# One high half of the split FFN weights made by VectorE instead of ScalarE

## The chip, the cores and the metric

The program runs on one core of one Trainium2 chip. Five engines work from queues of their own, each in the order of its queue: PE (TensorE, matmuls), DVE (VectorE), ACT (ScalarE), POOL (GpSimd) and SP (SyncE, which here only issues DMAs). An instruction that must wait for another engine or for a transfer holds up everything behind it on its own engine. The metric is the device time of one execution in microseconds (us), as the median of several runs.

## The reference

Four layers run over a sequence of 2048 rows of 512 columns: a state-space convolution and a gated feed-forward network (FFN), twice, each behind a layer norm and with a residual. All weights are float32 and shared by the two passes.

```
x = A_u
for _ in range(2):
    x = x + conv(layernorm(x))      # K[d, l] = Re sum_n C dt B exp(dt A l); causal FFT convolution, + u * Dskip
    x = x + ffn(layernorm(x))       # (silu(x @ w_gate) * (x @ w_up)) @ w_down, F = 1376
return x
```

## The kernel before

The sequence is cut into four blocks of 512 rows. The convolution kernel K is built in eight chunks of 64 columns (`gen_exp`, `gen_trig`, `gen_g`, `gen_e`, then the matmuls of `lags`, L496 and L497), taken to the frequency domain by matmuls (`spectra`, `first_parts`, `later_parts`) and kept as `w0r` for the first part and in DRAM (`wdr`) for the later ones. `ssm_half` multiplies a block's spectrum by it on DVE (L781, L784 into `yk`, then L786 and L787 into `yf`), turns the product back on PE (`pi`, L803), combines the pieces on ACT and DVE (`bb`, L753, L761, L762) and adds the result to the block (`xg`). The FFN then runs on PE over pairs of columns of F (`pgu`, L916 to L919, in two buffers; L883 to L885 for the last 96 columns), with ACT making silu (`sg`, L922), DVE the product with the up part (L923, which gives the `pgu` buffer free), ACT and DVE the two halves of the result (`hh` L924, `hl` L925), and PE the product with w_down (`py`, L931 to L933), which DVE adds to the block (L936).

The FFN multiplies in float16. So each weight is split once into two float16 tiles: a high half, the scaled weight rounded, and a low half, the scaled weight less the high half. `split_weights` (L652 to L700) makes lists of three kinds of step from eight pieces of w_gate and w_up (a quarter of the columns, 128 x 4 x 344, named by `j` = 0..3 and `wi` = 0 for gate, 1 for up) and eleven pieces of w_down: `load` issues the DMA into a float32 tile (`st`, or a part of `wsl`), `hi` makes the high half on ACT (L664 for gate and up, L689 for w_down), `lo` the low half on DVE (L669 and L692) from the loaded tile and the high half. The scales `sc6` are powers of two from the largest column norms; `scales()` computes them in a chain of small DVE instructions, of which L356 is the last.

What sets the order: from the start of the program up to the line `pscale = product_scale()` the instructions of PE, DVE, ACT and POOL stand in the order in which the code emits them (`tc.manual_schedule`). The end of that stretch, printed here, mixes the split with the last two chunks of K, the convolution of block 0 (`conv[0]` for the first 256 columns, `conv[1]` for the others; each `take` of one is a product on DVE and its turn back on PE) and the first norm (`first_norm`). `split(a, b)` emits the next `a` high halves, then the next `b` low ones. Behind that line, and for the DMA queue SP in parts of it too, a list scheduler that plays the program through with its own durations decides the order; a change in the stretch ahead can move everything behind it.

```
scales()
split(1, 0)              # hi of (j 0, gate)
first_parts(c, 0)        # PE L580, then ACT L581: w0r of q = 0
take(conv[0], 1)
split(1, 1)              # hi of (j 0, up), lo of (j 0, gate)
split(0, 0, 1)
first_parts(c - 1, 3)    # w0r of q = 3
split(1, 0)
take(conv[0], 1)
```

Of the kernel before, what the change touches and what calls it, by code (L numbers as in the profile page):

```python
# [15 lines left out]
AF = mybir.ActivationFunctionType  # L16
OP = mybir.AluOpType
# [57 lines left out]
def kernel(ctx, tc, x, a_re, a_im, b_re, b_im, c_re, c_im, log_dt, d_skip,  # L75
                           w_gate, w_up, w_down, c_ef, c_ei, c_ek, c_am, c_eh, c_eih, out):
    nc = tc.nc
    V, A, G, PE = nc.vector, nc.scalar, nc.gpsimd, nc.tensor
# [9 lines left out]
    def tl(shape, name, tag, dt=F32):  # L88
        return sb.tile(shape, dt, name=name, tag=tag, bufs=BUFS[tag])
# [544 lines left out]
    def wgu(wi, kc, lo, n=1):  # L634
        u = 8 * wi + 4 * lo + kc
        v = wsl[u // 6].rearrange("p (u f) -> p u f", u=6)
        return v[:, u % 6] if n == 1 else v[:, u % 6:u % 6 + n]

    def wd(fc, lo):
        r = 2 * fc + lo  # L640
        if r < 5:
            return wsl[2][:, 4 * F + r * D:4 * F + (r + 1) * D]
        return wsl[3][:, (r - 5) * D:(r - 4) * D] if r < 21 else wx

    def split_weights():


        cb = F // 4
        tags = iter(("bt", 0, 1, 2, "bt", 0, 1, 2, "n", "xf", "bt"))

        def columns(j, wi, src):
            fs = slice(j * cb, (j + 1) * cb)  # L652
            sc = sc6[:, wi:wi + 1]
            at = []

            def load():
                tag = next(tags)
                st = tl([P, 4, cb], "st2", tag) if isinstance(tag, str) else \
                    wsl[3].bitcast(F32)[:, 4 * cb * tag:4 * cb * (tag + 1)].rearrange("p (k f) -> p k f", k=4)
                nc.sync.dma_start(st, src[:, fs].rearrange("(k p) f -> p k f", p=P))  # L660
                at.append(st)

            def hi():
                A.activation(wgu(wi, 0, 0, 4)[:, :, fs], at[0], AF.Copy, scale=sc)  # L664

            def lo():
                n = 2 if wi == 0 else 4
                for k in range(0, 4, n):
                    V.scalar_tensor_tensor(wgu(wi, k, 1, n)[:, :, fs], at[0][:, k:k + n], sc,  # L669
                                           wgu(wi, 0, 0, 4)[:, k:k + n, fs], OP.mult, OP.subtract)  # L670
            return load, hi, lo

        def rows4(f0):
            n = min(4, F // P - f0)
            at = []

            def part(fc):
                rows = min(P, F - fc * P)
                sc = sc6[:rows, 2:3]

                def load():
                    st = tl([P, min(4, FT - f0), D], "st3", next(tags))
                    nc.sync.dma_start(st[:, :n], w_down[f0 * P:(f0 + n) * P].rearrange("(k p) d -> p k d", p=P))
                    if f0 + n < FT and n < 4:
                        nc.sync.dma_start(st[:F % P, n], w_down[(f0 + n) * P:])
                    at.append(st)

                def hi():
                    A.activation(wd(fc, 0)[:rows], at[0][:rows, fc - f0], AF.Copy, scale=sc)  # L689

                def lo():
                    V.scalar_tensor_tensor(wd(fc, 1)[:rows], at[0][:rows, fc - f0], sc, wd(fc, 0)[:rows],  # L692
                                           OP.mult, OP.subtract)
                return load if fc == f0 else None, hi, lo
            return [part(fc) for fc in range(f0, min(FT, f0 + 4))]

        parts = [columns(j, wi, src) for j in range(4) for wi, src in enumerate((w_gate, w_up))]
        for f0 in range(0, FT, 4):
            parts += rows4(f0)
        return [p[0] for p in parts if p[0]], [p[1] for p in parts], [p[2] for p in parts]  # L700
# [583 lines left out]
```

## Time and profile before

| what | value |
|---|---|
| median of 3 runs | 1151.85 us (1150.62 to 1154.33) |
| the profiled execution, its own time | 1153.06 us |
| its span, first to last instruction | 1151.3 us |
| instructions | 24412 |
| mean granted TensorE clock | 0.992 |

The page gives each engine's busy time and share of the span, the span in 40 slices, the chain of work that ended last and the costliest groups. The answers of the trace that the prediction shows are of four kinds. A row of the waits names who waited, for whom, and then the microseconds in total, how often, and the longest. A row of the timeline has the start in us, the duration, engine, line, operation, tiles written and read, shapes, how many instructions it merges, and in brackets the idle time before it with what ended it. A row of the groups by line gives, behind the bar, busy us and mean ns of one. A row of the windows gives, for a stretch of time, its length, then the busy time of PE, weight loads, DVE, ACT and POOL with counts, the granted clock of PE (1.00 is full speed), the DMA engines' share and GB/s. Times in the timeline count from the span's start; PE ends are modelled.

### The profile page before, as it was taken

How to read it: one execution, taken by the hardware profiler on the slowest of the kernel's cores; microseconds unless marked ns; L12 is line 12 of the kernel's file. 1: busy time of each engine (PE TensorE's matmuls, PEld its weight loads, DVE VectorE, ACT ScalarE, POOL GpSimd, SP SyncE). 2: the span in 40 equal slices, each digit the busy share in tenths (PEclk: the TensorE clock that was granted, in tenths of full speed). 3: DMA queues.
4: the chain of work that ended last, by engine and by line, in shares of the span. 5: the costliest groups of instructions: out<-in, count | busy, mean ns of one | idle time of the engine just before them, and what ended most of it. 6: DMA issues, size and time to landing. Idle time of an engine off the chain costs nothing.

```text
span 1151.3 us, 24412 instructions
## 1 busy us (share of the span) xinstructions
PE 1097.2 (95%) x9942; PEld 874.7 (76%) x9942; DVE 998.3 (87%) x1585; ACT 598.1 (52%) x1198; POOL 108.6 (9%) x163
## 2 busy tenths in 40 slices
PE   2989999999989999999999999999999999999998
PEld 1868888888875868686868687877778687876875
DVE  8999999988999899998999999989994999973211
ACT  6989998734454453567453534655434352334211
POOL 0112222210000100111010000110000100000000
PEclk9989999999989999999999999999999999999999
DMA  5367777868773355332354444334443156302000
GB/s 210 128 166 166 162 185 172 191 174 300 223 197 98 105 143 192 115 96 71 107 142 138 133 140 151 109 117 114 139 133 129 50 134 156 103 32 48 14 24 19
DMA packets 127314, 150.38 MB, mean 131 GB/s; under 512 B 50897, under 2 KB 75985, under 8 KB 127202
## 3 DMA queue, kind: packets, MB, share of 16 engines
q1 hardware_dynamic: 115298, 123.32, 35.6%
q0 software_dynamic: 11904, 25.50, 9.5%
q8 instruction: 78, 1.28, 0.5%
q14 instruction: 34, 0.28, 0.1%
HBM read 98.70 MB, written 33.82 MB: 115 GB/s over the span
## 4 chain that ended last, share of the span: by engine, by line
PE 39%; DVE 25%; issue 6%; DMA 2%; ACT 2%; POOL 1%; DVEq 0%; POOLq 0%; ACTq 0%
PE pgu L916 7%; PE pgu L917 7%; PE pgu L919 7%; PE py L931 4%; PE py L932 4%; PE py L933 4%; DVE yk L784 3%; DVE t L781 3%; PE pi L803 3%; DVE yk L781 3%; PE pf L280 2%; DMA mix<-nn 2%; DVE z L228 2%; DVE sg L923 2%; DVE hl L925 2%
## 5 line engine op out<-in xcount | busy, mean ns | idle before, releaser
L916 PE MATMUL pgu<-mix,wsl 128*128 128x256 f16 x1280 | 299.7, 273 | 5.6 <-DVE sg L923 4.7
L917 PE MATMUL pgu<-mix,wsl 128*128 128x256 f16 x1280 | 299.4, 273 | 0.0
L919 PE MATMUL pgu<-mix,wsl 128*128 128x256 f16 x1280 | 195.7, 273 | 0.0
L917 PEld LDWEIGHTS <-wsl 128*128 128x128 f16 x1280 | 125.5, 98 | 22.5 <-issue 6.2
L931 PE MATMUL py<-wsl,hh 128*128 128x512 f16 (+1 forms) x352 | 134.2, 381 | 7.0 <-DVE xg L936 5.3
L916 PEld LDWEIGHTS <-wsl 128*128 128x128 f16 x1280 | 125.5, 98 | 16.4
L919 PEld LDWEIGHTS <-wsl 128*128 128x128 f16 x1280 | 125.4, 98 | 14.8
L933 PE MATMUL py<-wsl,hl 128*128 128x512 f16 (+1 forms) x352 | 133.9, 381 | 0.0
L932 PE MATMUL py<-wsl,hh 128*128 128x512 f16 x320 | 122.0, 381 | 0.0
L781 DVE TENSOR_TENSOR t<-uu,w 128x1024 f32<-128x1024 f32 x96 | 117.0, 1218 | 0.2
L784 DVE TENSOR_TENSOR yk<-yk,t 128x1024 f32<-128x1024 f32 x96 | 116.9, 1218 | 0.2
L922 ACT ACTIVATE sg<-pgu,sc 128x512 f32<-128x512 f32 x80 | 54.6, 683 | 119.8 <-PE pgu L919 113.5
L923 DVE SCALAR_TENSOR_TENSOR sg<-pgu,sc,sg 128x512 f32<-128x512 f32 x80 | 59.7, 746 | 52.0 <-ACT sg L922 51.8
L924 ACT ACTIVATE hh<-sg 128x512 f16<-128x512 f32 x80 | 50.1, 627 | 80.6 <-DVE sg L923 80.6
L531 PE MATMUL pw<-kt,ek 128*128 128x256 f32 (+1 forms) x384 | 91.1, 374 | 0.0
L803 PE MATMUL pi<-yl,mix 128*128 128x256 f16 x576 | 78.9, 272 | 1.3 <-ACT yl L792 1.0
L531 PEld LDWEIGHTS pw<-kt,ek 128*128 128x128 f32 x384 | 72.6, 193 | 8.7
L280 PE MATMUL pf<-z,eh 128*128 128x256 f16 x576 | 74.9, 273 | 0.6 <-DVE z L228 0.6
L781 DVE TENSOR_TENSOR yk<-u,w0r 128x1024 f32<-128x1024 f32 x56 | 68.2, 1218 | 0.8 <-ACT u L282 0.8
L932 PEld LDWEIGHTS <-hh 128*128 128x128 f16 (+1 forms) x352 | 34.6, 98 | 44.1 <-issue 8.7
L496 PE MATMUL pk<-re,g 128*32 128x64 f32 x1024 | 65.1, 317 | 2.8 <-DMA g<-g 1.9
L925 DVE TENSOR_TENSOR hl<-sg,hh 128x512 f16<-128x512 f32 x80 | 54.8, 686 | 14.8 <-ACT hh L924 14.8
(238 smaller groups left out, 2158.7 us busy)
## 6 DMA issues: line engine op xcount, KB each, us to landing
uu<-udr SPq DMA_DIRECT2D x96, 256.0 KB, 3.0
w<-wdr SPq DMA_DIRECT2D x96, 256.0 KB, 2.7
udr<-u POOLq DMA_DIRECT2D x32, 256.0 KB, 2.7
g<-g POOLq DMA_DIRECT2D x6, 1024.0 KB, 9.0
udr<-u SPq DMA_DIRECT2D x16, 256.0 KB, 2.9
n<-xdr SPq DMA_DIRECT2D x4, 1024.0 KB, 5.6
kdr<-ks SPq DMA_DIRECT2D x6, 512.0 KB, 2.6
kt<-kdr SPq DMA_DIRECT2D x24, 128.0 KB, 3.0
```

The costliest lines, as they stand in the source:

```text
L280: PE.matmul(pf[:, o], lhsT=e, rhs=m, start=k == 0, stop=k == len(terms) - 1)
L531: PE.matmul(pw[:, i], lhsT=e, rhs=kt[:, :, c + 4 * k0:4 * k1:4, :].rearrange("p g k d -> p k g d"), start=c == 0, stop=c == 3)
L781: V.tensor_tensor(t, uu.unsqueeze(2).to_broadcast([P, NQ, 2, 2, DC]), w.unsqueeze(3).to_broadcast([P, NQ, 2, 2, DC]), OP.mult)
L784: V.tensor_tensor(yk, yk, t, OP.add)
L803: PE.matmul(pi[:, o], lhsT=e, rhs=m, start=k == 0, stop=k == len(terms) - 1)
L916: PE.matmul(o, lhsT=wgu(wi, k, 0)[:, fs], rhs=nh[:, k], start=k == 0, stop=False)
L917: PE.matmul(o, lhsT=wgu(wi, k, 1)[:, fs], rhs=nh[:, k], start=False, stop=False)
L919: PE.matmul(o, lhsT=wgu(wi, k, 0)[:, fs], rhs=nlo[:, k], start=False, stop=k == 3)
L923: V.scalar_tensor_tensor(sg, pgu[:, 1], sc6[:, 4:5], sg, OP.mult, OP.mult)
L931: PE.matmul(py[:, r], lhsT=hh[:n, f, rc], rhs=wd(f, 0)[:n], start=f == 0, stop=False)
L932: PE.matmul(py[:, r], lhsT=hh[:n, f, rc], rhs=wd(f, 1)[:n], start=False, stop=False)
L933: PE.matmul(py[:, r], lhsT=hl[:n, f, rc], rhs=wd(f, 0)[:n], start=False, stop=f == FT - 1)
```

## The change

The high half of the first piece (j = 0, gate) is no longer an ACT activation with a scale but one DVE multiplication of the loaded tile by the same scale; the other seven pieces of gate and up and all of w_down stay on ACT. The values are the same: a power of two times the weight, rounded to float16.

```diff
             def hi():
-                A.activation(wgu(wi, 0, 0, 4)[:, :, fs], at[0], AF.Copy, scale=sc)
+                if j == 0 and wi == 0:
+                    V.tensor_scalar(wgu(wi, 0, 0, 4)[:, :, fs], at[0], sc, None, OP.mult)
+                else:
+                    A.activation(wgu(wi, 0, 0, 4)[:, :, fs], at[0], AF.Copy, scale=sc)
```

The code grows by three lines, so a line behind L664 has a number that is three higher in the changed kernel (L781 becomes L784, L923 becomes L926). In the rows below, `x128x4x344` and the like are the shapes written.

DVE, behind the chain of the scales, before (`sc_92` are the scales, `st_2529` the loaded piece, `wsl_2661` and `wsl_2662` the tiles of the halves):

```order
L356 TENSOR_SCALAR sc_92<-bits 128x6
L781 TENSOR_TENSOR yk<-mix,w0r 128x1024
L786 TENSOR_TENSOR yf<-yk 128x256
L787 TENSOR_TENSOR yf<-yk 128x256
L669 SCALAR_TENSOR_TENSOR wsl_2661<-st_2529,sc_92,wsl_2661 128x2x344
L669 SCALAR_TENSOR_TENSOR wsl_2662<-st_2529,sc_92,wsl_2661 128x2x344
```

and now:

```order
L356 TENSOR_SCALAR sc_92<-bits 128x6
L665 TENSOR_SCALAR wsl_2661<-st_2529,sc_92 128x4x344
L784 TENSOR_TENSOR yk<-mix,w0r 128x1024
L789 TENSOR_TENSOR yf<-yk 128x256
L790 TENSOR_TENSOR yf<-yk 128x256
L672 SCALAR_TENSOR_TENSOR wsl_2661<-st_2529,sc_92,wsl_2661 128x2x344
L672 SCALAR_TENSOR_TENSOR wsl_2662<-st_2529,sc_92,wsl_2661 128x2x344
```

One instruction is put in directly behind the scales, ahead of the third product of `conv[0]`. On ACT the activation between the copy of K (L525) and the copy of the first `w0r` (L581) is gone; the rest of ACT's order in the stretch written by hand is kept.

Behind that stretch the scheduler's order changes too. DVE at the first FFN groups, before, directly behind `bb<-bb,pi` (L761; `bb` is a piece of block 1's convolution, `pi` its second turned-back product, `sg` the product of the first FFN group):

```order
L784 TENSOR_TENSOR yk<-yk,t 128x1024
L614 TENSOR_TENSOR sy<-sy,dmax 1x1
L228 SCALAR_TENSOR_TENSOR xg<-bb_2671,xg 128x256
L228 SCALAR_TENSOR_TENSOR xg<-t_3009,xg 128x256
L692 SCALAR_TENSOR_TENSOR wsl_2664<-st_3056,sc_92,wsl_2664 128x512
L669 SCALAR_TENSOR_TENSOR wsl_2661<-wsl_2664,sc_92,wsl_2661 128x2x344
L669 SCALAR_TENSOR_TENSOR wsl_2662<-wsl_2664,sc_92,wsl_2661 128x2x344
L600 TENSOR_TENSOR wos<-pw,wos 128x2x3x64
L669 SCALAR_TENSOR_TENSOR wsl_2663<-wsl_2664,sc_92,wsl_2662 128x4x344
L600 TENSOR_TENSOR wos<-pw,wos 128x2x3x64
L762 TENSOR_TENSOR bb<-bb,pi 128x512
L923 SCALAR_TENSOR_TENSOR sg_3086<-pgu,sc_92,sg_3086 128x512
```

and now:

```order
L695 SCALAR_TENSOR_TENSOR wsl_2664<-st_3056,sc_92,wsl_2664 128x512
L834 TENSOR_TENSOR bb_2671<-bb_2671 128x256
L926 SCALAR_TENSOR_TENSOR sg_3086<-pgu,sc_92,sg_3086 128x512
L835 TENSOR_TENSOR t_3009<-t_3009,t_3010 128x256
L764 TENSOR_TENSOR bb<-bb,pi 128x512
L787 TENSOR_TENSOR yk<-yk,t 128x1024
L228 SCALAR_TENSOR_TENSOR xg<-bb_2671,xg 128x256
L228 SCALAR_TENSOR_TENSOR xg<-t_3009,xg 128x256
L672 SCALAR_TENSOR_TENSOR wsl_2661<-wsl_2664,sc_92,wsl_2661 128x2x344
```

The first `sg` product moves from behind the low halves to a place ahead of `bb<-bb,pi`, and so does the first low half of w_down (L692). The second `sg` product stays behind the low halves, the two `wos` and `t`; the third, which stood behind the two `hl` rows, `nn` and a `yk`, now stands ahead of all of these but one `hl`.

PE, where that `pi` is made. Before it stood inside the first FFN group:

```order
L919 MATMUL pgu<-mix,wsl_2661 128x256
L803 MATMUL pi<-yf_2955,mix 128x256
L919 LDWEIGHTS wsl_2661
L919 MATMUL pgu<-mix,wsl_2661 128x256
L803 MATMUL pi<-yf_2955,mix 128x256 x3
```

Now it stands behind the end of the first group, one matmul into the second:

```order
L922 MATMUL pgu<-mix,wsl_2662 128x256
L806 MATMUL pi<-yf_2955,mix 128x256
L919 LDWEIGHTS wsl_2661
L919 MATMUL pgu<-mix,wsl_2661 128x256
L806 MATMUL pi<-yf_2955,mix 128x256 x3
```

It moved by 14 FFN matmuls. In the same way the third `pi` moved from inside the third group to behind it, and the fourth to behind the group of the last columns. ACT, at the end of block 0's kernel work, before (`ks<-kt` is L607, the last reader of the tile whose place the second load of w_down takes):

```order
L598 ACTIVATE wos<-w0r 128x64
L753 ACTIVATE bb<-pi 128x512
L599 ACTIVATE wos<-pw 128x2x64
L598 ACTIVATE wos<-w0r 128x64
L599 ACTIVATE wos<-pw 128x2x64
L607 ACTIVATE ks,wsum<-kt_429 128x1024
L689 ACTIVATE wsl_2664<-st_3056,sc_92 128x512
```

and now:

```order
L599 ACTIVATE wos<-pw 128x2x64
L607 ACTIVATE ks,wsum<-kt_429 128x1024
L756 ACTIVATE bb<-pi 128x512
L692 ACTIVATE wsl_2664<-st_3056,sc_92 128x512
L925 ACT_TABLE_LOAD
L925 ACTIVATE sg_3086<-pgu,sc_92 128x512
```

The copy `bb<-pi` went from ahead of L607 to behind it. Further on, the order differs in many small places on all engines.

## The prediction

> **What bounds the kernel now.** I read the page's engines first, then the busy time by stretches, then PE's waits ahead of the stretch that is full. The waits are those of the 110 us from 256 to 366, where the moved work lies.
>
> ```profile
> PE 1097.2 (95%) x9942; PEld 874.7 (76%) x9942; DVE 998.3 (87%) x1585; ACT 598.1 (52%) x1198; POOL 108.6 (9%) x163
> 366.00:1008.00 642.00, 634.30 (x5341) 494.04 (x5339) 603.19 (x1008) 302.89 (x586) 50.23 (x62) 1.00 0.42 123
> 1010.00:1138.00 128.00, 127.65 (x1046) 96.19 (x1043) 45.18 (x74) 34.77 (x64) 1.80 (x4) 1.00 0.09 25
> PE pgu L916 <- DVE sg L923: 4.7, 1, 4.7
> PE py L931 <- DVE xg L936: 2.3, 1, 2.3
> PE pt L850 <- ACT nn L848: 2.3, 1, 2.3
> PE pi L803 <- DVE yf L786: 1.2, 1, 1.2
> 320.90:327.80 6.90, 5.12 (x23) 3.67 (x23) 6.90 (x14) 6.72 (x13) 0.70 (x1) 0.51 0.44 135
> 361.90:365.30 3.40, 3.40 (x9) 1.21 (x9) 3.40 (x7) 3.37 (x11) 0.16 (x1) 0.50 0.42 114
> ```
>
> PE carries the end. Behind 366 it is busy 634.30 of 642.00 us, then 127.65 of 128.00; little can be saved or hidden there, and a shift of PE at 366 reaches the end nearly whole. Ahead of it PE stands still four times for DVE or ACT: 1.2, 2.3, 4.7 and 2.3, together 10.5 us. Two of the waits are followed by a stretch at half clock (0.51 for 6.9 us with 5.12 busy, 0.50 for 3.4). At half clock half of the busy time is lost: 2.5 and 1.7 us. So 10.5 + 4.2 = 14.7 us is all that any change of order here can win.
>
> **The instruction itself.** First the rows that price it, then those beside its place.
>
> ```profile
> 254.37 0.17 DVE L356 TENSOR_SCALAR sc<-bits 128x6 int32<-128x6 int32 x1
> 241.67 0.37 SPq L660 DMA_DIRECT2D st<-in_B_w_gate_dram  x1
> st<-in_B_w_gate_dram SPq DMA_DIRECT2D x2, 688.0 KB, 9.0
> L382 DVE TENSOR_SCALAR th<-ft 128x448 int32<-128x448 f32 x1 | 0.4, 394 | 0.0
> L382 DVE TENSOR_SCALAR th<-ft 128x64 int32<-128x64 f32 x1 | 0.2, 195 | 0.0
> 262.88 1.78 DVE L669 SCALAR_TENSOR_TENSOR wsl<-st,sc,wsl 128x688 f16<-128x688 f32 x2 [6.37 <-ACT wsl L664]
> 261.41 1.43 ACT L664 ACTIVATE wsl<-st,sc 128x1376 f16<-128x1376 f32 x1
> ```
>
> The piece was asked for at 241.67 and lands some 9.0 us later, near 250.7, ahead of the scales, which are done at 254.5. So the new instruction starts behind L356 at once. The trace has none of 128 x 1376 with one scale. The two L382 rows give 199 ns for 384 more elements, 0.52 ns each; from 195 ns at 64 that is 0.87 us at 1376. Dearer is two passes of L669 over 688 elements each, 1.78 us together. I take 0.87, the same kind of operation. Either way **the cost is nothing**: DVE stood for 6.37 us ahead of L669, and even 1.78 fits. Without that cover it would be 0.9 to 1.8 us on DVE. ACT's 1.43 us falls away; that gains nothing by itself, as ACT's next copy waits for PE (`[1.27 <-PE pw L580]`, below).
>
> **What DVE gains in the stretch written by hand.**
>
> ```profile
> 260.35 1.99 PE L803 MATMUL pi<-yf,mix 128*128 128x256 f32 x8
> 264.11 0.28 ACT L581 ACTIVATE w0r<-pw 128x128 f32<-128x128 f32 x1 [1.27 <-PE pw L580]
> 266.57 0.68 DVE L761 TENSOR_TENSOR bb<-bb,pi 128x512 f32<-128x512 f32 x1
> 267.73 0.37 ACT L581 ACTIVATE w0r<-pw 128x256 f32<-128x256 f32 x1
> 267.89 1.22 DVE L781 TENSOR_TENSOR yk<-mix,w0r 128x1024 f32<-128x1024 f32 x1
> 270.00 1.23 DVE L781 TENSOR_TENSOR yk<-mix,w0r 128x1024 f32<-128x1024 f32 x1
> ```
>
> L669 needed the high half until 262.88; now both of its parts run behind `yf`, at 257.4 to 259.1, the next `yk` and `yf` to 261.0, and DVE waits for the turned-back product (PE is done with it at 260.35 + 1.99 = 262.34) instead of for ACT. `bb` is done at 263.7, not 267.2. But the two next `yk` need the `w0r` copies, which hang on PE: the one at 267.89 can start at 264.11 + 0.28 = 264.4, the one at 270.00 not ahead of 267.73 + 0.37 = 268.1. So of the 6.4 us **1.9 us remain**, 270.00 less 268.1. Behind that DVE runs without a gap to the norm of block 0; the wait of 1.2 us for `yf` goes, that of 2.3 for `nn` starts and ends 1.9 sooner: PE, ACT and DVE are all 1.9 us ahead at 301. SP's next gate load and the load of `xg` go out sooner too; neither is waited for here.
>
> **What the new order makes of it.** First ACT and SP, then DVE, then PE.
>
> ```profile
> 306.66 0.60 ACT L753 ACTIVATE bb<-pi 128x512 f32<-128x512 f32 x1 [2.73 <-DVE t L228]
> 307.61 1.07 ACT L607 ACTIVATE ks<-kt 128x1024 f32<-128x1024 f32 x1
> 308.84 0.38 SPq L683 DMA_DIRECT2D st<-in_B_w_down_dram  x1
> 314.23 0.72 ACT L689 ACTIVATE wsl<-st,sc 128x512 f16<-128x512 f32 x1 [5.46 <-DMA st<-in_B_w_down_dram]
> 314.97 1.28 ACT L922 ACT_TABLE_LOAD   x1
> 316.26 0.69 ACT L922 ACTIVATE sg<-pgu,sc 128x512 f32<-128x512 f32 x1
> 313.98 0.68 DVE L761 TENSOR_TENSOR bb<-bb,pi 128x512 f32<-128x512 f32 x1
> 316.45 0.73 DVE L692 SCALAR_TENSOR_TENSOR wsl<-st,sc,wsl 128x512 f16<-128x512 f32 x1
> 321.89 0.73 DVE L923 SCALAR_TENSOR_TENSOR sg<-pgu,sc,sg 128x512 f32<-128x512 f32 x1
> 335.85 0.73 DVE L923 SCALAR_TENSOR_TENSOR sg<-pgu,sc,sg 128x512 f32<-128x512 f32 x1
> 340.13 0.69 DVE L869 TENSOR_TENSOR nn<-nn 128x512 f16<-128x512 f32 x1 [1.75 <-DMA mix<-nn]
> 358.97 1.22 DVE L784 TENSOR_TENSOR yk<-yk,t 128x1024 f32<-128x1024 f32 x1
> 360.44 0.68 DVE L761 TENSOR_TENSOR bb<-bb,pi 128x512 f32<-128x512 f32 x1
> 361.04 0.74 DVE L936 SCALAR_TENSOR_TENSOR xg<-py,sc,xg 128x512 f32<-128x512 f32 x1
> 317.38 0.60 PE L919 MATMUL pgu<-mix,wsl 128*128 128x256 f16 x4
> 332.12 0.27 PE L916 MATMUL pgu<-mix,wsl 128*128 128x256 f16 x1
> 337.36 0.21 PE L883 MATMUL pgu<-wsl,mix 128*128 128x96 f16 x1
> ```
>
> ACT: L607 stood behind `bb<-pi`, which waited 2.73 for DVE. Ahead of it, and 1.9 sooner, it ends near 304.6; so the w_down load goes out at 304.75 instead of 308.84. With the 314.23 − 308.84 = 5.4 us that it took, it lands at 310.15. Then come L689 0.72, the table load 1.28, silu 0.69 and the first L923 0.73: done near 313.65, where before it was 322.6.
>
> PE: the second group, with `pi` ahead of most of it, ends near 316.0 (317.98 less the 1.9). The third then starts at once: the wait of 4.7 is gone and the half clock with it. A group takes 337.36 − 332.12 = 5.24; the third ends at 321.2, a `pi` and 1.1 of wait for its `yf` follow, the fourth runs 324.35 to 329.6 (before, 332.12 to 337.36).
>
> DVE decides how much of it stays. L761 starts at 314.0 as before, now behind L692 and the first L923. Before, 21.87 gapless us lay from 313.98 to the third L923 at 335.85. Moved out of them are L692 and a L923 (0.73 each), one `yk` (1.22), one `nn` and one `hl` (0.69 each) and some 0.2 of small ones: 4.2, less about 0.07 for each big row, since a row starts that much ahead of its forerunner's end (360.44 + 0.68 against 361.04): 3.9. So the third L923 runs at 332.0 to 332.75, and PE, ready at 329.6, gets **a new wait of 3.1 us** at L883. PE is 4.6 ahead there. From the third L923 to L936, 25.19 us before, 2.4 of the moved rows come in and 2.34 go (L784, a `t` and L761 now stand behind L936: 361.04 − 358.97 = 2.07, and a small one of 0.27), and the wait of 1.75 for the transposed `nn` changes by −0.3 to +0.4. L936 starts at 357.3 to 358.0, and `py` goes on near 358.05 instead of 361.84: **3.8 us ahead**, behind a wait of 2.4 as before. I take 0.4 less for a load that lands a little later than its forerunner, since DVE is held by it one to one: **3.4 us** at 366.
>
> In this execution's own time that is 1153.06 − 3.4 = 1149.7. It lies 1.2 above the median; the step is the same from the median, 1151.85 − 3.4 = **1148.4**, the forecast.
>
> [...] Half clock came behind a wait of 4.7, but also behind one of 2.3, as the windows show. [...]
>
> **The rivals.**
>
> ```profile
> x<-in_A_u_dram SPq DMA_DIRECT2D x1, 1024.0 KB, 9.8
> ```
>
> - *More is kept* (0.27). [...] Were the 1.9 won, and the 4.7, 2.5, 2.3 and 1.7 gone as well, the gain is 13.1 and the time 1138.7. Against that: DVE's rows between the third L923 and L936 stay as many as they were.
> - *The new wait brings half clock* (0.10). It starts at 332.75 and costs 1.7 to 2.5, say 2.0, as far as the wait of 2.4 behind it does not swallow it: 1151.85 − 3.4 + 2.0 = 1150.4.
> - *Given back* (0.10). Behind 362 both PE and DVE are full and the order differs in many places; if DVE or a transfer there sets the pace (DVE is busy 603.19 of 642.00), or the instruction does not free DVE because the piece lands late, the time stays 1151.85.
> - *The load of w_down holds DVE: slower* (0.08). L692 and the first L923 now stand ahead of the chain of `bb`, `yk` and the low halves, so a late landing delays all of it. The first 3.4 us of delay behind 310.15 use up the gain, and some 0.4 more is lost in the wait: the point is a landing at 314.0, 9.3 us behind its issue. The largest time for 1024 KB in the trace is 9.8: landing at 314.55, DVE 0.55 late, the wait at L883 7.5 us long and half clock of 2.5 behind it: 1151.85 + 0.55 + 2.5 = 1154.9. Against it: the same load took 5.4 four microseconds later.
>
> **How the numbers follow.** The forecast has 0.45, with gains of 2.4 to 4.6 us (1147.2 to 1149.5). The range reaches up to 1153.0, over "given back" and half way into the slower case, and down to 1143.5, over the smaller half of "more is kept". The price of the instruction, 0.87 or 1.78, moves nothing. 0.3% is 3.5 us, about what a measurement of this kernel can tell from no change. The forecast lies on that line, so half of it, 0.22, is faster, with 0.26 of "more is kept": 0.48. The rest, 0.23 + 0.01 + 0.10 + 0.10, is 0.44 within 0.3%; 0.08 is slower.
>
> **What would show it.** In the changed kernel's trace: the new row on DVE at about 0.87 us and no wait of 6.4 for ACT; `pt` of block 0's norm 1.9 us sooner, at 293.0; the w_down load issued near 304.8 and landed near 310; no 4.7 at the third group and clock 1.00 from 320 to 328; instead a wait of about 3 at the last columns' group (L886 now) for a product `sg`; `py` going on near 358. The prediction fails if DVE is held by another wait in the 1.9, if that load lands behind 313, if clock 0.5 stands behind 332, or if PE shows new waits behind 366.

## The result, and the profile after

| | before | after |
|---|---|---|
| median | 1153.51 us (1150.62 to 1155.47, 6 runs) | 1148.82 us (1147.92 to 1149.88, 6 runs) |
| ratio after / before | | 0.9961 (95% interval 0.9946 to 0.9977) |
| the profiled execution: time, span | 1153.06, 1151.3 us | 1149.31, 1147.5 us |

The kernel is 4.5 us faster (0.39%, interval 2.7 to 6.2 us). The forecast was 1148.4, a gain of 3.4 from the 1151.85 that three runs had given. Over six runs the kernel before has 1153.51, so the time was met more closely than the gain.

First the page's engines, the stretch that is full, and PE's waits from 250 to 366 in the changed kernel, in the same form as before.

```profile
PE 1095.6 (95%) x9942; PEld 874.1 (76%) x9942; DVE 998.9 (87%) x1586; ACT 596.5 (52%) x1197; POOL 113.6 (10%) x163
366.00:1008.00 642.00, 634.23 (x5372) 495.14 (x5371) 606.63 (x1012) 303.57 (x587) 53.51 (x62) 1.00 0.42 124
PE pi L806 <- DVE yf L789: 3.6, 2, 3.1
PE pgu L886 <- DVE sg L926: 3.0, 1, 3.0
PE pt L853 <- ACT nn L851: 1.9, 1, 1.9
PE pgu L919 <- DVE sg L926: 0.7, 1, 0.7
PE py L934 <- DVE xg L939: 0.7, 1, 0.7
```

PE has as much to do as before and the stretch behind 366 is as full. The waits ahead of it are 9.9 us together, where they were 10.5: the 4.7 for `sg` is down to 0.7, but 3.0 stand at the last columns and 3.1 at a `pi`. By that list hardly anything was won. The gain shows in the times, here from DVE, PE, SP and ACT of the changed kernel (timeline rows; for lines behind L664 the number of before is three lower).

```profile
254.39 0.94 DVE L665 TENSOR_SCALAR wsl<-st,sc 128x1376 f16<-128x1376 f32 x1
262.54 0.69 DVE L764 TENSOR_TENSOR bb<-bb,pi 128x512 f32<-128x512 f32 x1 [1.57 <-PE pi L806]
264.51 1.23 DVE L784 TENSOR_TENSOR yk<-mix,w0r 128x1024 f32<-128x1024 f32 x1 [0.56 <-ACT w0r L581]
268.21 1.23 DVE L784 TENSOR_TENSOR yk<-mix,w0r 128x1024 f32<-128x1024 f32 x1 [1.69 <-ACT w0r L581]
293.08 1.36 PE L853 MATMUL pt<-ident,nn 128*128 128x128 f32 x8 [1.89 <-ACT nn L851]
302.84 0.44 SPq L727 DMA_DIRECT2D eh<-in_c_eh_dram  x1
304.81 0.38 SPq L686 DMA_DIRECT2D st<-in_B_w_down_dram  x1
313.38 0.72 ACT L692 ACTIVATE wsl<-st,sc 128x512 f16<-128x512 f32 x1 [7.89 <-DMA st<-in_B_w_down_dram]
314.14 0.75 DVE L695 SCALAR_TENSOR_TENSOR wsl<-st,sc,wsl 128x512 f16<-128x512 f32 x1 [2.42 <-ACT wsl L692]
316.14 0.75 DVE L926 SCALAR_TENSOR_TENSOR sg<-pgu,sc,sg 128x512 f32<-128x512 f32 x1 [0.91 <-ACT sg L925]
335.15 0.74 DVE L926 SCALAR_TENSOR_TENSOR sg<-pgu,sc,sg 128x512 f32<-128x512 f32 x1
359.65 0.38 PE L934 MATMUL py<-wsl,hh 128*128 128x512 f16 x1 [0.67 <-DVE xg L939]
468.54 0.74 DVE L939 SCALAR_TENSOR_TENSOR xg<-py,sc,xg 128x512 f32<-128x512 f32 x1
```

The new row is there, and DVE's wait of 6.4 us for ACT is three waits of 1.6, 0.6 and 1.7 for PE and the `w0r` copies: `pt` starts 1.8 us sooner (294.88 before). The load goes out 4.0 us sooner, but ACT gets its tile at 313.38, 8.6 us behind the issue instead of 5.4, and DVE stands for it twice. So the third `sg` is only 0.7 us sooner than before and `py` goes on 2.2 sooner. One block further, at the first `xg` behind `py`, the lead is 4.4. In the kernel before, the load of `eh` and that `xg` stood here:

```profile
303.90 0.38 SPq L724 DMA_DIRECT2D eh<-in_c_eh_dram  x1
...
472.94 0.74 DVE L936 SCALAR_TENSOR_TENSOR xg<-py,sc,xg 128x512 f32<-128x512 f32 x1
```

Between `py` and that `xg` lies the stretch at half clock of before from 361.9 on (0.50, PE busy for all 3.4 us), which cost PE 1.7 us; in this execution of the changed kernel the clock is full there (1.00 from 358 to 366 and from 366 to 1008).

### The profile page after: what moved, and what is told of

The parts are those of the page before. It is cut to its first block, busy times and chain, and to the rows that moved or that the text cites. A ratio compares the mean times of both kernels' runs of the same rounds, so it can differ in the third digit from the quotient of the medians.

```text
span 1147.5 us, 24410 instructions
## 1 busy us (share of the span) xinstructions
PE 1095.6 (95%) x9942; PEld 874.1 (76%) x9942; DVE 998.9 (87%) x1586; ACT 596.5 (52%) x1197; POOL 113.6 (10%) x163
## 4 chain that ended last, share of the span: by engine, by line
DVE 33%; PE 25%; issue 9%; DMA 4%; ACT 3%; POOL 1%; SPq 1%; DVEq 0%; ACTq 0%; POOLq 0%
DVE t L784 5%; DVE yk L787 4%; PE pgu L919 4%; PE pgu L920 4%; PE pgu L922 4%; DVE z L228 3%; DVE yk L784 3%; PE py L934 3%; PE py L935 3%; PE py L936 3%; DVE sg L926 2%; DVE hl L928 2%; PE pi L806 2%; DMA mix<-nn 2%; DVE bb L228 1%
## 5 line engine op out<-in xcount | busy, mean ns | idle before, releaser
L936 PE MATMUL py<-wsl,hl 128*128 128x512 f16 (+1 forms) x352 | 133.4, 379 | 0.0
L784 DVE TENSOR_TENSOR t<-uu,w 128x1024 f32<-128x1024 f32 x96 | 116.8, 1216 | 0.2
L926 DVE SCALAR_TENSOR_TENSOR sg<-pgu,sc,sg 128x512 f32<-128x512 f32 x80 | 59.6, 745 | 53.0 <-ACT sg L925 52.9
L531 PE MATMUL pw<-kt,ek 128*128 128x256 f32 (+1 forms) x384 | 91.0, 374 | 0.0
L531 PEld LDWEIGHTS pw<-kt,ek 128*128 128x128 f32 x384 | 72.5, 193 | 8.6
L784 DVE TENSOR_TENSOR yk<-u,w0r 128x1024 f32<-128x1024 f32 x56 | 68.1, 1215 | 0.0
```

Of the source, the lines that this page charges most:

```text
L531: PE.matmul(pw[:, i], lhsT=e, rhs=kt[:, :, c + 4 * k0:4 * k1:4, :].rearrange("p g k d -> p k g d"), start=c == 0, stop=c == 3)
L784: V.tensor_tensor(t, uu.unsqueeze(2).to_broadcast([P, NQ, 2, 2, DC]), w.unsqueeze(3).to_broadcast([P, NQ, 2, 2, DC]), OP.mult)
L926: V.scalar_tensor_tensor(sg, pgu[:, 1], sc6[:, 4:5], sg, OP.mult, OP.mult)
L936: PE.matmul(py[:, r], lhsT=hl[:n, f, rc], rhs=wd(f, 0)[:n], start=False, stop=f == FT - 1)
```

## The experiments

The scheduler answers every edit with another order. So all but the op's two places are held in these kernels: each names, for every engine, its instructions in the order of the kernel before or of the changed one, and neighbours in it get a dependency that orders them and waits for nothing.

```diff
+    for engine, names in ORDER:
+        for a, b in zip(names, names[1:]):
+            tc.add_manual_dep(b, a, mybir.DependencyInfo(mybir.DependencyClass.NoSync, ...))
```

Single rows can then be moved by hand. Lines in these kernels are numbered as in the kernel before. Ratios are to runs of the kernel before on the same chip; 0.001 is 1.15 us. Runs 1 to 4, 5 to 8 and 9 to 12 were on one chip each.

| run | ratio | 95% interval | `py` goes on: its `xg` starts at |
|---|---|---|---|
| the change | 0.9961 | 0.9946 to 0.9977 | 358.86 |
| 1 op alone | 0.9978 | 0.9969 to 0.9987 | 358.44 |
| 2 order alone | 0.9977 | 0.9967 to 0.9986 | 359.37 |
| 3 DVE rows behind | 0.9937 | 0.9926 to 0.9949 | 355.85 |
| 4 `eh` behind | 0.9938 | 0.9924 to 0.9951 | 356.32 |
| 5 L607 back | 0.9979 | 0.9970 to 0.9988 | 359.30 |
| 6 `sg` early | 0.9973 | 0.9962 to 0.9984 | 358.00 |
| 7 op three times | 0.9972 | 0.9962 to 0.9983 | 357.56 |
| 8 both | 0.9954 | 0.9942 to 0.9967 | 356.83 |
| 9 the change again | 0.9963 | 0.9951 to 0.9976 | 358.05 |
| 10 op nine times | 1.0004 | 0.9995 to 1.0013 | 362.67 |
| 11 `eh` late | 0.9950 | 0.9937 to 0.9962 | 355.93 |
| 12 third `sg` early | 0.9952 | 0.9938 to 0.9966 | 357.18 |

Before, that `xg` starts at 361.04 in the profile.

### 1 and 2: the op without the order, the order without the op

```diff
 # 1: hi() as in the changed kernel
-ORDER of the changed kernel
+ORDER of the kernel before
 # 2: hi() as in the kernel before
-ORDER of the kernel before
+ORDER of the changed kernel
```

> The change's one instruction, with every other instruction of every engine held in the order of the kernel before. The prediction's first step alone: DVE and PE 1.9 us ahead at 301 (pt of the first norm near 293.0), the w_down load issued 1.9 sooner (near 306.9), the 4.7 us wait at the third FFN group still there. [...] Rival (the gain is the new order's alone): 0 to 0.5 us faster.

> The high half back on ACT as before, with every other instruction of every engine held in the order of the changed kernel. Theory (the parts add up): pt of the first norm at 294.9 as before, the w_down load issued near 306.7, no wait of 4.7 at the third FFN group, no half clock behind 320; about 2 us faster than before, 1.9 slower than the changed kernel. Rival (the order gains only where DVE has been freed): no faster than before.

The op alone is 2.5 us faster (interval 1.5 to 3.6), where the prediction's first step has 1.9, the order alone 2.7 (1.6 to 3.8); together 5.2, and the change has 4.5. The parts add up within what was measured. Both rivals fall: the op's gain doesn't need the order, nor the order the op. In 1 the wait of 4.7 at the third group is still there; in 2 `pt` starts at 294.59 and that wait is gone. In its profile a stretch of half clock came behind the norm: from 295.98 on two rows of `pw` (L531) took 0.85 and 2.13 us, where the rows of the same shapes behind 300 took 0.49 and 1.14. The mean clock was 0.994, in the change's profile 0.997; by an estimate from these two that is some 3.4 us lost, of which this stretch has about 1.8. Where the rest lay is not shown, so it stays open whether the words on the clock in the second expectation held. The w_down load went out at 307.99, not near 306.7.

### 7 and 10: the cover of the op

```diff
-V.tensor_scalar(wgu(wi, 0, 0, 4)[:, :, fs], at[0], sc, None, OP.mult)
+[V.tensor_scalar(wgu(wi, 0, 0, 4)[:, :, fs], at[0], sc, None, OP.mult) for _ in range(3)]   # 7; range(9) in 10
```

> The changed kernel's order with the new DVE instruction issued three times in a row (the same result each time). Theory (it lies under a wait): 0.86 us each, so DVE comes 1.7 us later to bb, where it stood 1.6 us for PE, and then still waits for both w0r copies; pt of the first norm at the same time, no change against the changed kernel (within 0.3 us). Rival (DVE is full there, the instruction costs what it takes): 1.7 us slower.

> The changed kernel's order with the new DVE instruction issued nine times in a row: 8 x 0.97 = 7.8 us more ahead of the product yk. Theory (cover of a bounded size): yf comes at 265.0, where PE started its pi at 260.2 and yf had been ready at 257.3, so 2.9 us of cover are used up and 4.8 remain; pt of the first norm near 297.9, 4 to 5 us slower than the changed kernel. Rival A (no cover, each costs what it takes): 7.8 slower. Rival B (the waits for w0r and at the norm swallow more): under 2 slower.

Timeline rows of run 7, then of run 10:

```profile
254.29 2.88 DVE L664 TENSOR_SCALAR wsl<-st,sc 128x1376 f16<-128x1376 f32 x3
264.50 1.23 DVE L781 TENSOR_TENSOR yk<-mix,w0r 128x1024 f32<-128x1024 f32 x1 [0.39 <-ACT w0r L581]
293.06 1.36 PE L850 MATMUL pt<-ident,nn 128*128 128x128 f32 x8 [1.88 <-ACT nn L848]
```

```profile
254.10 8.72 DVE L664 TENSOR_SCALAR wsl<-st,sc 128x1376 f16<-128x1376 f32 x9
264.47 1.99 PE L803 MATMUL pi<-yf,mix 128*128 128x256 f32 x8 [0.40 <-DVE yf L786]
296.63 1.48 PE L850 MATMUL pt<-ident,nn 128*128 128x128 f32 x8 [2.18 <-ACT nn L848]
```

By the trace two more copies change nothing: the wait of 1.57 for `pi` has become DVE's work and `pt` starts at 293.06 as with one. The medians alone don't tell this from the rival's 1.7: the ratio is 1.3 us above the change's, and the intervals overlap. Eight more put 7.8 us on DVE; `pi` now waits for `yf`, PE runs some 4 us late, `pt` 3.6 (4.8 were expected), and the kernel is 3.9 us slower than the change beside it (1151.97 against 1148.09). So this place takes up to some 4 us more of DVE time for nothing, where the op needs 0.94.

### 3, 4, 11 and 9: what made the w_down load late

```diff
 # 3: DVE, behind yk<-u,w0r and wmax
-wsl<-st,sc,wsl      (first low half of w_down)
 bb<-bb
-sg<-pgu,sc,sg       (first FFN group)
 t<-t,t
 bb<-bb,pi
 yk<-yk,t
 xg<-bb,xg
 xg<-t,xg
+wsl<-st,sc,wsl
 wsl<-wsl,sc,wsl
+sg<-pgu,sc,sg
 # 4: SP
-eh<-in_c_eh_dram
 wdr<-mix
 st<-in_B_w_down_dram
+eh<-in_c_eh_dram
 # 11: SP, eh behind the third load of w_down instead; 9: as the changed kernel
```

> The changed kernel's order, but on DVE the first low half of w_down and the first sg product stand behind work that is ready (bb, yk, two residual rows, one low half), so that DVE does not stand for the w_down load. Theory (the late load costs the changed kernel 3.3 us, DVE one to one): the DVE waits of 2.4 and 0.9 near 312 to 316 go, py goes on near 356.3 instead of 359.65, 3 us faster than the changed kernel. Rival (PE, ACT or the transposes set the pace there): waits move, py within 1 us of 359.65, no change against the changed kernel.

> The changed kernel's order, but on SP the 768 KB load of eh (issued 2.0 us ahead of the w_down load) is issued behind it. Theory (the load took 8.5 us instead of 5.4 because it now shares the DMA engines with eh): the w_down load lands 5.4 to 6 us behind its issue, the DVE waits near 312 to 316 shrink by 2.5 to 3, 2 to 3 us faster than the changed kernel. Rival (other transfers hold it, or the queue): it still takes 8 us or more, no change against the changed kernel.

> The changed kernel's order with eh issued behind the third w_down load, some 12 us later than in e4_eh_behind, DVE's order as it is. Theory (eh beside the w_down load makes it late, and DVE is held one to one): the w_down load takes 5.0 to 5.5 us, DVE's waits there come to 0.3 or less, py goes on near 356.5; 3 to 4 us faster than the changed kernel beside it. Rival (the lateness was chance, it changes from execution to execution): within 1 us of the changed kernel beside it.

> The changed kernel once more, its order held as it stands, as the control on the chip of the three runs beside it. All theories: 1148.8 give or take 1, 0.996 of before; the w_down load takes 7 to 8.6 us where eh is issued 2 us ahead of it; PE waits of 3 for DVE at the third pi and at the last columns.

Run 4: the two issues, ACT when the tile is there, the first and third `sg`, and `xg`.

```profile
304.88 0.38 SPq L683 DMA_DIRECT2D st<-in_B_w_down_dram  x1
305.31 0.49 SPq L724 DMA_DIRECT2D eh<-in_c_eh_dram  x1
310.85 0.72 ACT L689 ACTIVATE wsl<-st,sc 128x512 f16<-128x512 f32 x1 [5.29 <-DMA st<-in_B_w_down_dram]
313.60 0.75 DVE L923 SCALAR_TENSOR_TENSOR sg<-pgu,sc,sg 128x512 f32<-128x512 f32 x1 [0.82 <-ACT sg L922]
332.62 0.73 DVE L923 SCALAR_TENSOR_TENSOR sg<-pgu,sc,sg 128x512 f32<-128x512 f32 x1
356.32 0.73 DVE L936 SCALAR_TENSOR_TENSOR xg<-py,sc,xg 128x512 f32<-128x512 f32 x1
```

With `eh` (768 KB) behind it the load, issued at the same time as in the change, is there after 6.0 us, and all that follows comes 2.5 sooner: the third `sg` at 332.62, where the forecast had 332.0. From issue to ACT's start the load took 8.6 and 8.2 us in the two profiles of the change, 7.5 and 7.3 in runs 3 and 7 (`eh` 2.0 to 2.6 us ahead in all four), and 6.0, 5.9, 5.6 and 5.5 in the four with `eh` behind it (4, 8, 11, 12): that is no chance. `eh` itself landed 7.0 us behind its issue in the profiles of before and of the change, so 2.1 us of it lay behind the issue of the load before and 5.0 in the change. With `eh` 4.6 to 4.9 us ahead it took 5.4 (before), 6.1 and 6.0 (runs 1 and 6); in between, at 2.7 to 3.8, it varied: 5.9, 7.2 and 7.7 (runs 2, 10, 5). Run 3 leaves the load late (ACT starts on it at 312.75) and takes DVE out of its way; it gains the same. Against the change's 0.9961 and 0.9963 (the second from another chip) runs 3 and 4 are 2.6 to 3.0 us faster; of the 3.3 us that DVE stood there, most comes back. Run 11 was 2.2 us faster by its median than the change beside it (1145.88 against 1148.09), 1.5 by the ratios, whose intervals overlap; 3 to 4 were expected. In the profiles `xg` is 2.1 apart (358.05 against 355.93), as the change's own load was somewhat earlier in that execution.

### 6 and 12: what a wait of PE is worth

```diff
 # 6: on run 1, DVE
 wsl<-wsl,sc,wsl
+sg<-pgu,sc,sg       (first FFN group)
 wsl<-wsl,sc,wsl
 wos<-pw,wos
 wsl<-wsl,sc,wsl
 wos<-pw,wos
 bb<-bb,pi
-sg<-pgu,sc,sg
 # 12: on run 11, DVE, sg of the third group
+sg<-pgu,sc,sg
 wsl<-st,sc,wsl      (twice, and wx<-st,sc,wsl)
-sg<-pgu,sc,sg
```

> The op alone with the order of before (as e1_op_only), but on DVE the first sg product stands behind the first low half of the last gate and up piece instead of behind the low halves, wos and bb. Theory (DVE's row of work decides, not PE's wait): the wait of 4.7 at the third FFN group shrinks to about 1 and comes back as 3 to 4 us at the last columns' group, which still starts near 334.5; py goes on near 359.2; 0 to 0.7 us faster than e1_op_only, more only by a stretch of half clock. Rival (what PE no longer waits it keeps): about 4 us faster than e1_op_only.

> As e11_eh_late, and on DVE the third sg product ahead of the last three low halves of w_down. Theory (DVE's rows up to the first product of py decide): PE's wait of 3 at the last columns shrinks to 1 and comes back later, py goes on within 0.5 us of e11_eh_late, no change against it (within 0.7). Rival (a PE wait and the half clock behind it are worth what they last): 2 us faster than e11_eh_late or more.

PE's waits from 300 to 362 in runs 1, 6, 11 and 12, in this order:

```profile
PE pgu L916 <- DVE sg L923: 5.1, 2, 4.7
PE py L931 <- DVE xg L936: 2.3, 1, 2.3
```

```profile
PE pgu L883 <- DVE sg L923: 3.3, 1, 3.3
PE py L931 <- DVE xg L936: 2.2, 1, 2.2
PE pi L803 <- DVE yf L786: 1.9, 1, 1.9
PE pgu L916 <- DVE sg L923: 0.8, 1, 0.8
```

```profile
PE pgu L883 <- DVE sg L923: 3.0, 1, 3.0
PE pi L803 <- DVE yf L786: 0.9, 1, 0.9
```

```profile
PE pi L803 <- DVE yf L786: 3.4, 2, 2.5
PE pgu L883 <- DVE sg L923: 1.0, 1, 1.0
```

Run 6 takes 3.9 us of the wait at L916 away, and 3.3 stand at L883, 1.9 at `pi`. `xg` starts 0.4 sooner than in run 1, and the ratio is better by 0.0005, 0.6 us, of which nothing is sure. In run 12 the wait at L883 went from 3.0 to 1.0 and that at `pi` from 0.9 to 3.4, and the time did not change (0.9950, 0.9952). Its `xg` came 1.25 later than in run 11, where at most 0.5 was expected; the load was there for ACT later by the same 1.25 (311.70 against 310.45). PE's waits here are DVE's backlog wherever PE meets it: removing one moves it.

Time lost to the clock went the same way where PE had such a wait still ahead of it. In run 9 half clock lay ahead of L883 (0.50 from 323.60 to 327.00, PE busy for 2.42 us, so 1.2 lost in that stretch), and the wait there was 0.5 instead of the change's 3.0. In run 4 the wait of 3.0 at L883 was followed by 6.8 us at half clock, as one rival of the prediction had it for the changed kernel:

```profile
332.52:339.35 6.83, 5.95 (x53) 5.58 (x53) 6.83 (x12) 3.95 (x7) 0.20 (x1) 0.50 0.61 186
```

PE is busy for 5.95 us of it, so 3.0 are lost. DVE is busy for all of it and has no gap up to `xg` at 356.32, 4.7 us ahead of before and 0.4 behind run 11. But PE stands for no `xg` there, in run 4 or in run 11 (mean clocks 0.994 and 0.995, by an estimate from these some 1.1 us more lost in run 4): the `py` at 351.56 is 1.6 behind run 11's, and the next `xg`, at 409.88, still 1.3 (408.54). So in that profile the loss was not hidden.

### 5 and 8: one not settled, one missed

```diff
 # 5: ACT, on the change's order
-ks<-kt              (L607)
 bb<-pi
+ks<-kt
 # 8: runs 3 and 4 together, with the first low half and the first sg ahead of yk<-yk,t
```

> The changed kernel's order, but on ACT the reader of kt (L607) back behind the copy bb<-pi, as it was before; that copy can end at 305.5, so the w_down load is issued near 306.2 instead of 304.8. Theory (the load shares the DMA engines with what was issued ahead of it, so an earlier issue gains nothing): it lands within 0.5 us of the changed kernel's 313.4, py goes on within 0.5 us of 359.65, no change against the changed kernel. Rival (the term of the prediction: each us of issue is a us of landing): 1.4 us later landing, DVE one to one, 1.4 us slower than the changed kernel.

> The changed kernel's order with eh issued behind the w_down load (as e4_eh_behind) and DVE's rows so placed that it doesn't stand there (as e3_dve_behind, the first sg product somewhat earlier). Theory (both take away the same wait of DVE): the last 0.8 us of DVE's idle time goes, nothing more: third sg near 331.8, 0.3 to 1 us faster than either, 7.5 to 8 us faster than before. Rival (two gains that add): 6 us faster than the changed kernel, 10.5 faster than before.

In 5 the load went out at 306.16, 1.35 later, and ACT started on it at 313.83, 0.45 later; measured from `pt`, which was 0.43 sooner in that execution, it is 0.9 for an issue 1.8 later. The theory had 0.5, the rival as much as the issue, and the medians don't separate: 0.9979 is 2 us slower than the change, with intervals that overlap. How much of L607's earlier place is kept stays open. Run 8 was to be the fastest and is slower than 3 and 4 by 1.9 us. In its profile PE ran at half clock from 293.64 on (0.50 up to 297.06), `w0r`'s copies and L607 came later, and the load was issued at 306.42 instead of 304.88. Run 12 has such a stretch at the same place (six matmuls of `pw`, L531, took 2.00 us from 295.16 on), runs 3, 4 and 11 have not (1.14). Whether that explains the medians was not tried.

The fastest are runs 3 and 4, 7.2 us faster than before: one row moved on the DMA queue, or two on DVE.

## Why the prediction came out right, and where it didn't

| step | forecast | profile after |
|---|---|---|
| new row on DVE | 0.87 | 0.94 |
| `pt` of the first norm | 293.0 | 293.08 |
| w_down load issued | 304.75 | 304.81 |
| the load is there for ACT | 310.15 | 313.38 |
| third FFN group starts | 316.0 | 316.94 |
| third `sg` | 332.0 | 335.15 |
| wait at the last columns | 3.1 | 3.0 |
| `py` goes on | 358.05 | 359.65 |
| half clock behind 362 | as before (1.7) | none |

*The instruction and its cover* were right: by the traces it cost nothing, also when tripled. *The 1.9 us* were right, with both waits for `w0r` where they were forecast; run 1, 2.5 us faster (1.5 to 3.6), shows that the op's gain reaches the end without the order. Its profile also has less half clock than that of before (mean clock 0.995 against 0.992), so it can't show that all of the 2.5 comes from these 1.9.

*The order* was right in its parts and wrong in one size. The step "with the 314.23 − 308.84 = 5.4 us that it took, it lands at 310.15" failed: the load took 8.6. It was moved up 4.0 us in the queue while `eh` ahead of it moved only 1.1, so that it was issued 2.0 us behind `eh` instead of 4.9; runs 4 and 11 give the 5.5 to 6.0 back. The chain behind it was right, DVE one to one: the third `sg` came 3.15 late for a load 3.2 late. A load behind 313 was one of the prediction's own signs of failure, and it came. The forecast's rival "the load of w_down holds DVE" named this mechanism with 314.0 as the point from which it would lose; the load came at 313.4, short of it.

Of the 3.2 us about half came back ahead of `py`, because DVE's wait of 1.75 for the transposed `nn` had gone under it. So the lead at `py` was 2.2 instead of 3.8. The sum still met the result since 1.7 came from the half clock that was to stay: part of the rival "more is kept". 2.2 + 1.7 and some 0.5 make the 4.4 at 470 (the 0.5 were not followed up). Two errors of 1.6 and 1.7 cancelled, which was luck: the forecast had allowed 0.4 for a late load, and without the second it would have been 1.2 too hopeful by the profile. How much of the 1.7 the medians have is open: the six runs of the change had mean clocks of 0.992 to 0.997, and the profiled one 0.997. One sum of the prediction was a little off: 332.0 + 25.19 + 2.4 − 2.34 and −0.3 to +0.4 give L936 at 357.0 to 357.7, not 357.3 to 358.0; its `py` at 358.05 fits the former.

*The new wait* of 3.1 came, and a second one of 3.1 at a `pi`, where 1.1 was forecast, as DVE was later. Neither brought half clock in this execution (1.00 from 78.35 to 1146.71). In run 9, the same order of instructions, half clock came with the wait at that `pi`, 3.06 us in both (0.50 from 323.60 on; next section but one). What makes the difference no run shows, so the chances that the prediction gave to half clock were its author's estimate.

*Given back behind 366* did not happen: at the `xg` rows (L936 before) the lead is 4.4 us at 473, at most 5.1, at 537, and 4.0 at the end.

## What to carry to other kernels

Where two engines are both full, add up the rows of the one that the other waits for up to the next common point; a wait that is removed there is worth only what shortens that row of work (in run 6 a wait became 3.9 us shorter and the time 0.6, of which nothing is sure; in run 12 one became 2.0 shorter and the time did not change). When a transfer moves up in its queue, don't take its old duration with it: look at what was issued just ahead of it, and whether that moved too (here 5.4 us became 8.6, with `eh` issued 2.0 us ahead instead of 4.9). And hold the scheduler's order while testing, or every edit is also another order.

## What the hardware showed

*Half clock after like waits.* In the profile of before the granted clock was 0.50 for 6.83 us from 71.76 on, for 6.83 from 320.94 and for 3.41 from 361.90, and 1.00 between these stretches and behind them up to 1150; in that of the change it was 0.50 for 6.83 from 71.52 on and 1.00 from 78.35 to 1146.71. The matmuls of one `py` (128x512 written) started 0.43 us apart in the stretch from 361.90, and 0.22 apart behind it. Four stretches of 3.41 us at full clock, of before, run 9, the change and run 8 (second number: PE's busy time in it):

```profile
358.49:361.90 3.41, 1.13 (x27) 1.03 (x24) 3.41 (x7) 3.08 (x10) 0.00 (x0) 1.00 0.20 68
```

```profile
320.19:323.60 3.41, 1.34 (x13) 0.96 (x10) 3.41 (x6) 3.41 (x8) 0.00 (x0) 1.00 0.94 334
```

```profile
320.67:324.08 3.41, 1.67 (x16) 1.25 (x13) 3.41 (x5) 3.41 (x9) 0.00 (x0) 1.00 0.88 313
```

```profile
290.23:293.64 3.41, 1.52 (x11) 1.15 (x9) 3.38 (x7) 1.36 (x2) 1.34 (x1) 1.00 0.10 13
```

Behind the first the clock was 0.50 from 361.90 to 365.31, behind the second from 323.60 to 327.00, behind the fourth from 293.64 to 297.06. Behind the third it stayed at 1.00 (324.08 to 327.50). Over the end of the second and of the third stretch PE waited for `yf`, up to 324.58 and 325.40, 3.06 us in both, in one order of instructions; and for `nn` 1.89 us in run 8 (`pt` at 293.15) and 1.89 in the change (`pt` at 293.08), where the clock then was 1.00 (293.40 to 296.80). So in these executions the length of the wait did not decide; what did is not shown.

*The scatter goes with it.* Of 56 runs of the kernel before on three chips, the 28 with a mean clock of 0.994 took 1151.3 us on average, the 17 with 0.992 took 1153.1. One stretch of 3.41 us at 0.50 is 0.0015 of the mean of 1151 us, and a PE that is busy throughout, as from 361.90 on in the profile of before, loses 1.7 us in it. No run changed the clock alone, so that the one makes the other is not shown. That a profile shows such a stretch doesn't mean that the median has it.
